# Attention and a gated feed-forward block on one core: bias rows of the first two heads computed in place, the others by DMA, and two loads issued by another engine

## The chip, the cores and the metric

The kernel runs on one core of a Trainium2 chip. A core has TensorE (PE; its weight loads are the row PEld), VectorE (DVE), ScalarE (ACT), GpSimd (POOL) and SyncE (SP), which only issues and waits, and 16 DMA engines. The metric is device time in microseconds: the median of several runs of one launch. The kernel before took 376.75 us (three runs, 376.2 to 377.3).

## The reference

Sixty-four heads (8 batches of 8) of causal attention over 576 positions with head size 64. Each head has a row of selection values s; the running sum of their positive parts is a bias on the scores. The result goes through a gated feed-forward block of width 1536.

```python
scores = scale * np.matmul(q, k.transpose(0, 1, 3, 2))
cum = np.cumsum(np.maximum(s, 0.0), axis=-1)
bias = -(cum[:, :, :, None] - cum[:, :, None, :])
scores = np.where(causal, -1000000000.0, scores + np.minimum(bias, 0.0))
attn = softmax(scores)                       # exp, divided by the sum
x = (attn @ v) rearranged to 4608 tokens x 512
g = x @ w_gate
out = (g * sigmoid(g) * (x @ w_val)) @ w_out
```

## The kernel before

**Scores with the bias inside the product.** A head's q and k are held transposed: 64 partitions of head dimension, 576 positions along the free axis. The other 64 partitions of the same operand tile are free, and four rows of them carry the bias: the running sum, split into a bf16 part and the bf16 rest, against rows of constants. One matmul with a contraction of 128 then gives score plus bias. The operand tiles are KQ[i][r] (kq in the profile). A group of four heads ("head batch" hb) uses the pair KQ[hb % 2]; r = 0 holds heads 0 and 1 of the group side by side, r = 1 heads 2 and 3. With r = 0 the data is in partitions 0 to 63 and the bias rows begin at partition 64; with r = 1 it is the other way round.

**The bias rows.** s (64 heads, one per partition) is loaded by SyncE (L188). VectorE makes, for all heads at once, 8 times the positive part (L226), the running sum c8 (L227, a scan), its bf16 part (L230), the rest (L231) and a copy for the other side (L232), into HL: one partition per head, four rows of two sides. `aug(hb, engs)` (L178 to L186) then moves each head's line of HL into the four rows of its operand by one small DMA, 9 KB per head. The rest of those 64 partitions has to be zero; ScalarE, GpSimd and VectorE fill it at the start (L213 to L220).

**The start.** SyncE issues s, then k and q of head batch 0 in halves ("rows" r = 0, 1); GpSimd issues k and q of batch 1 (L221). A half is cast to bf16 (L247), transposed by TensorE (L293) and copied out of PSUM to KQ (`pe_out`, L305) by ScalarE or VectorE. The order is written out by hand in L905 to L975: fillers for TensorE (`keep_warm`), casts, `aug(0)`, rows of batch 0, the loads of v (`load_v`) and of the weights by GpSimd, `aug(1)`, casts of batch 1, scores of heads 0 to 3 with the transposes of batch 1 between them, `aug(2)`, scores 4 and 5, the products with v (`values`), and so on. After `aug(3)` SyncE issues v of batch 1 and k, q of head batches 4 and 5 (L957 to L959).

**After the start** attention and feed-forward are interleaved. `ffn_items(tt)` (L870) is a generator of steps for 512 tokens: for each of 12 feature tiles a gate block and a value block (L629, four matmuls each), with ScalarE's tanh (L650) and VectorE's `pp` (L652, empties the gate's bank) and `ht` (L663, empties the value's bank); then the output product (L686 or L735). The main loop (L1003 to L1033) counts these steps as items, lets `pump` advance the attention generator in proportion, and calls what was hung on an item by `at_item(n, f)`. Blocks are numbered here as items are: gate block of tile ft is item 2 ft + 1, value block item 2 ft + 2. In the chunks named below, a head's scores are four pieces with their own banks (`score_piece`, L338), followed by ScalarE's exponential (L369).

**What fixes the order.** Each engine runs its instructions in the order in which the program gives them, and waits in order too. Every DMA that SyncE issues goes to one queue (q1 in the profile), all of GpSimd's to another (q0). PSUM has eight banks, chosen at build time (`take`, L120): a block that takes a bank waits for the engine that last emptied it.

Of the kernel before, what the change touches and what calls it, by code (L numbers as in the profile page):

```python
# [12 lines left out]
FP32 = mybir.dt.float32  # L13
BF16 = mybir.dt.bfloat16
# [5 lines left out]
def kernel(  # L20
# [20 lines left out]
    HB = 4  # L41
# [55 lines left out]
    one_s = const.tile([128, 1], FP32)  # L97
    HL = const.tile([BH, 4, 2, S], BF16)
    XR = 3 * TT
# [4 lines left out]
    first = first_sbuf.enter_context(tc.tile_pool(name="first", bufs=1))  # L104
    s_sb = first.tile([BH, S], FP32)
    c8 = first.tile([BH, S], FP32)
    PTP = {0: first, "bufs": 7}
    lower = first.tile([128, 512], BF16)

    with tc.manual_schedule():  # L110
# [25 lines left out]
        def load_one(hb, name, rs=(0, NR), eng=nc.sync):  # L136
            b, g = divmod(hb, 2)
            if rs[0] == 0:
                loaded[name, hb] = raw.tile([128, NR, J, D], FP32, tag="raw" + name, name="raw" + name)
            eng.dma_start(  # L140
                loaded[name, hb][:, rs[0] : rs[1], :, :].rearrange("x r j d -> x r (j d)"),
                SRC[name][0][b, g * HB + 2 * rs[0] : g * HB + 2 * rs[1], :, :].rearrange(
                    "(r e) (p j) d -> (e p) r (j d)", e=2, j=J
                ),
            )
# [28 lines left out]
        def aug_rows(i, r):  # L174
            r0 = 64 * (1 - r)
            return KQ[i][r][r0 : r0 + 64, :, :].bitcast(FP32)

        def aug(hb, engs):  # L178
            for hh in range(HB):
                r, e = divmod(hh, 2)  # L180
                r0 = 64 * (1 - r)
                bh = hb * HB + hh
                engs[hh].dma_start(  # L183
                    KQ[hb % 2][r][r0 : r0 + 4, :, e * S : (e + 1) * S],
                    HL[bh : bh + 1, :, :, :],
                )  # L186

        nc.sync.dma_start(s_sb, s.rearrange("b h n -> (b h) n"))  # L188
        def init_vt(i):
# [3 lines left out]
        for r in range(NR):  # L193
            load_one(0, "k", (r, r + 1))
            load_one(0, "q", (r, r + 1))

        nc.vector.memset(warm, 0.0)
        nc.vector.memset(one_s, 1.0)
        nc.scalar.activation(warm, warm, AF.Exp)
        nc.vector.memset(HL[:, 0:2, 0, :].bitcast(FP32), ONES2)  # L200
        nc.vector.memset(HL[:, 2:4, 1, :].bitcast(FP32), NEGS2)
        make_identity(nc, ident)
# [3 lines left out]
            compare_op=ALU.is_ge, fill=nc.gpsimd.to_reg(MASKED), base=0, channel_multiplier=-1,  # L206
        )

        def pads(i):
            for r in range(2):  # L210
                nc.gpsimd.memset(KQ[i][r][64 * r : 64 * r + 64, :, NR * S :], 0.0)  # L211

        for r in range(2):  # L213
            nc.gpsimd.memset(aug_rows(0, r)[:, 1, :], 0.0)
            nc.scalar.mul(
                KQ[0][r][64 * (1 - r) : 64 * (1 - r) + 64, 0, :],
                one_s[0:64, 0:1].to_broadcast([64, NR * S + 64]), 0.0,
            )
        pads(0)
        nc.vector.memset(aug_rows(1, 0), 0.0)  # L220
        for nm in ("k", "q"):  # L221
            load_one(1, nm, eng=nc.gpsimd)
        init_vt(0)
        pads(1)

        nc.vector.tensor_scalar(s_sb, s_sb, 0.0, 8.0, ALU.max, ALU.mult)  # L226
        nc.vector.tensor_tensor_scan(  # L227
            c8, one_s[0:BH, 0:1].to_broadcast([BH, S]), s_sb, 0.0, ALU.mult, ALU.add
        )
        nc.vector.tensor_copy(HL[:, 0, 1, :], c8)  # L230
        nc.vector.tensor_sub(HL[:, 1, 1, :], c8, HL[:, 0, 1, :])  # L231
        nc.vector.tensor_copy(HL[:, 2:4, 0, :], HL[:, 0:2, 1, :])  # L232

# [650 lines left out]

        def row_half(nm, r, eng):
            for g in range(2):
                pe_transpose_half(0, nm, g, r)
            for g in range(2):
                pe_out(0, nm, g, r, eng)
# [17 lines left out]
        cast_half(0, "q", 0, nc.scalar)  # L907
        aug(0, SP4)
        row_half("k", 0, nc.scalar)
        row_half("q", 0, nc.vector)  # L910
        cast_half(0, "k", 1, nc.scalar)
        cast_half(0, "q", 1, nc.gpsimd)
        nc.gpsimd.memset(aug_rows(1, 1), 0.0)
        load_v(0, range(5), nc.gpsimd)
        w_load("g", 0)
        aug(1, SP4)
        keep_warm(10)
        row_half("k", 1, nc.scalar)
        row_half("q", 1, nc.vector)
        keep_warm(10)  # L920
        cast_one(1, "k", nc.vector)
        cast_one(1, "q", nc.vector)
        for c in range(3):
# [8 lines left out]
        load_one(3, "k", eng=nc.gpsimd)  # L932
        scores(0)
        half_batch("k")
        scores(1)
        half_batch("q")
        scores(2)
        scores(3)
        for nm in ("k", "q"):
            for g in range(2):  # L940
                pe_out(1, nm, g, 1, nc.vector)
        cast_v(0, 4, nc.vector)
        aug(2, SP4)
        cast_one(2, "k", nc.gpsimd)
# [52 lines left out]

        at_item(2, prep_one, 2, 2)
        at_item(8, cast_one, 3, "k", nc.gpsimd)
        at_item(9, cast_one, 3, "q", nc.gpsimd)  # L1000
# [64 lines left out]
```

## Time and profile before

| | us |
|---|---|
| median of 3 runs | 376.75 (376.2 to 377.3) |
| the profiled execution, its own time | 375.79 |
| its span, first to last instruction | 374.0 |
| TensorE busy, 0 to 10 / 10 to 20 / 20 to 30 / 30 to 40 | 7.38 / 8.00 / 9.92 / 8.02 |
| TensorE busy, 40 to 50 / 50 to 60 / 60 to 70 | 9.81 / 9.62 / 9.89 |
| TensorE busy in each 50 us from 100 to 350 | 49.58 to 49.84 |
| VectorE busy, 40 to 50 / 50 to 60 / 60 to 70 / 70 to 80 | 7.52 / 7.21 / 6.91 / 2.85 |

A row of a timeline gives the start and length in us, the engine, the line, the operation, what it writes and reads, the number of merged instructions, and in brackets the idle time of the engine before it and what ended it. In a "waits" line the name after the arrow is what ended the wait. SPq rows are issues by SyncE's queue: their length is the time of issuing, not of the transfer. "Landing" is when a transfer's data is all there.

### The profile page before, as it was taken

Reading aid. Unit: us, or ns where it says so; the run is one execution under the profiler, and the core shown is the slowest. Engines: PE = TensorE matmul, PEld = TensorE weight load, DVE = VectorE, ACT = ScalarE, POOL = GpSimd, SP = SyncE. Lnnn points to the kernel's source line nnn. Section 1 sums busy time; section 2 is a strip of 40 time slices with the busy share of each in tenths; the row PEclk is TensorE's granted clock in tenths of the full one; section 3 lists DMA queues with packets and bytes.
Section 4 is the critical chain, followed back from the end, with each engine's and each line's share of the span. In section 5 each row is a group of like instructions: output and inputs, shape, how many; then the busy total and the mean of one; then the engine's idle time right before and its main releaser. Section 6 shows DMA issues by size and latency. Waiting matters only on the chain.

```text
span 374.0 us, 8759 instructions
## 1 busy us (share of the span) xinstructions
PE 360.7 (96%) x3259; PEld 230.6 (62%) x3300; DVE 289.6 (77%) x578; ACT 240.4 (64%) x471; POOL 212.3 (57%) x325
## 2 busy tenths in 40 slices
PE   7799899999999999999999999999999999999995
PEld 6584456655555556855685559655865585476464
DVE  8968776468995899588967997699858867975984
ACT  8777677698876877588757875686566523323321
POOL 8883555856455647494649464955675516315320
PEclk9999999999999999999999999999999999999999
DMA  7899999799877997896779675984132103002003
GB/s 239 193 258 253 219 257 267 237 303 247 245 186 220 254 262 196 178 281 205 211 167 266 178 182 174 255 206 98 40 119 62 35 19 128 2 0 95 20 0 114
DMA packets 97146, 64.23 MB, mean 172 GB/s; under 512 B 77232, under 2 KB 82736, under 8 KB 97104
## 3 DMA queue, kind: packets, MB, share of 16 engines
q1 hardware_dynamic: 84976, 41.46, 45.2%
q0 software_dynamic: 12128, 22.21, 22.6%
q8 instruction: 26, 0.43, 0.5%
q14 instruction: 16, 0.13, 0.1%
HBM read 37.90 MB, written 19.86 MB: 154 GB/s over the span
## 4 chain that ended last, share of the span: by engine, by line
PE 85%; DMA 6%; POOL 5%; ACT 1%; issue 1%; DVE 1%; DVEq 0%; POOLq 0%; ACTq 0%
PE bank L629 45%; PE bank L735 17%; PE bank L359 10%; PE bank L396 7%; PE bank L686 5%; DMA rawk<-in_k_dram 4%; DMA rawv<-in_v_dram 2%; POOL rawv L157 1%; POOL vt L168 1%; POOL wv L332 1%; ACT pt L369 1%; PE bank L287 0%; POOL rawq L140 0%; ACT kq L314 0%; POOL kq L211 0%
## 5 line engine op out<-in xcount | busy, mean ns | idle before, releaser
L369 ACT ACTIVATE pt<-bank 128x512 bf16<-128x512 f32 (+1 forms) x256 | 120.4, 510 | 31.0 <-PE bank L359 18.2
L629 PE MATMUL bank<-XT,wg 128*128 128x512 bf16 x418 | 110.3, 379 | 1.2 <-DVE pp L652 0.3
L629 PE MATMUL bank<-XT,wv 128*128 128x512 bf16 x412 | 109.3, 379 | 1.1
L650 ACT ACTIVATE th<-bank 128x512 bf16<-128x512 f32 x108 | 64.7, 599 | 55.9 <-PE bank L629 53.6
L652 DVE SCALAR_TENSOR_TENSOR pp<-th,bank 128x512 bf16<-128x512 bf16 x108 | 73.6, 682 | 19.2 <-ACT th L650 18.7
L663 DVE SCALAR_TENSOR_TENSOR ht<-pp,bank 128x512 bf16<-128x512 bf16 x108 | 74.1, 686 | 10.6 <-PE bank L629 0.4
L359 PE MATMUL bank<-kq 128*128 128x128 bf16 (+4 forms) x576 | 75.6, 240 | 1.5 <-DMA kq<-HL 1.0
L672 POOL TENSOR_TENSOR ht<-ht 128x512 bf16<-128x512 bf16 x35 | 40.4, 1154 | 52.2 <-DVE su L670 52.1
L359 PEld LDWEIGHTS <-kq 128*128 128x128 bf16 x576 | 45.8, 98 | 31.5 <-issue 1.9
L629 PEld LDWEIGHTS <-wv 128*128 128x128 bf16 x432 | 38.4, 98 | 36.5 <-issue 0.6
L629 PEld LDWEIGHTS <-wg 128*128 128x128 bf16 x432 | 38.3, 98 | 34.2 <-issue 0.7
L396 PEld LDWEIGHTS <-pt 128*128 128x128 bf16 x960 | 41.9, 98 | 17.2
L374 POOL TENSOR_SCALAR_AFFINE_SELECT pt<-pt 128x512 bf16<-128x512 bf16 x56 | 36.8, 658 | 27.3 <-ACT pt L369 22.7
L396 PE MATMUL bank<-vt,pt 128*128 128x65 bf16 x960 | 47.0, 194 | 0.4 <-POOL vt L168 0.3
L430 POOL DMA_DIRECT2D xs<-ot x24 | 21.7, 905 | 30.0 <-DVE ot L413 27.6
L735 PEld LDWEIGHTS <-ht 128*128 128x128 bf16 x336 | 31.2, 98 | 4.3
L413 DVE TENSOR_TENSOR ot<-bank,rc 128x320 bf16<-128x320 f32 x64 | 31.5, 492 | 2.2
L183 POOL DMA_DIRECT2D kq<-HL x48 | 28.9, 604 | 0.0
L735 PEld LDWEIGHTS <-su 128*128 128x128 bf16 x252 | 23.5, 98 | 3.3
L686 PE MATMUL bank<-wo,ht 128*128 128x512 bf16 x90 | 24.8, 379 | 0.3
L800 POOL TENSOR_TENSOR ysb<-ysb 128x512 f32<-128x512 f32 x12 | 15.2, 1270 | 15.3 <-DVE ysb L794 15.3
L379 POOL TENSOR_SCALAR_AFFINE_SELECT pt<-pt 128x64 bf16<-128x64 bf16 x56 | 14.8, 264 | 15.8 <-ACT pt L369 15.7
(93 smaller groups left out, 384.6 us busy)
## 6 DMA issues: line engine op xcount, KB each, us to landing
out_dram<-ysb POOLq DMA_DIRECT2D x32, 256.0 KB, 4.5
rawv<-in_v_dram SPq DMA_DIRECT2D x28, 256.0 KB
rawk<-in_k_dram SPq DMA_DIRECT2D x12, 576.0 KB
rawq<-in_q_dram SPq DMA_DIRECT2D x12, 576.0 KB
xs<-ot POOLq DMA_DIRECT2D x24, 160.0 KB, 3.5
ks<-ck SPq DMA_DIRECT2D x11, 288.0 KB
qs<-cq SPq DMA_DIRECT2D x11, 288.0 KB
rawk<-in_k_dram POOLq DMA_DIRECT2D x3, 576.0 KB, 7.3
```

The lines of the kernel that those rows point to most:

```text
L359: nc.tensor.matmul(sc[:, o : o + w], T[:, 1, e * S + 128 * tj : e * S + 128 * (tj + 1)], T[:, 0, e * S + lo : e * S + hi], start=not maske ...
L369: nc.scalar.activation(pt[:, c0 : c0 + n], sc, AF.Exp, scale=0.125)
L374: nc.gpsimd.affine_select(pt[:, 1088:1600], pt[:, 1088:1600], pattern=[[0, 4], [1, 128]], compare_op=ALU.is_ge, fill=zreg, base=0, channel ...
L396: nc.tensor.matmul(av[:, bi * (D + 1) : (bi + 1) * (D + 1)], pt[:, c0 : c0 + 128], VT[b % 2][:, tj, h, :], start=(tj == 0), stop=(tj == bi),)
L413: nc.vector.tensor_mul(ot[:, :, e * D : (e + 1) * D], av3[:, :, 0:D], rc[:, :, None].to_broadcast([128, NCH, D]),)
L629: nc.tensor.matmul(view(bs, TT), w[:, c, f0 : f0 + 128], xt[:, c, :], start=(c == 0), stop=(c == 3),)
L650: nc.scalar.activation(th, pg, AF.Tanh, scale=0.5)
L652: nc.vector.scalar_tensor_tensor(pp, in0=th, scalar=1.0, in1=pg, op0=ALU.add, op1=ALU.mult)
L663: nc.vector.scalar_tensor_tensor(hp[:, 2 * k2 : 2 * k2 + 2, :].rearrange("p a n -> p (a n)"), in0=pp, scalar=0.5, in1=pv, op0=ALU.mult, op ...
L672: (nc.vector if ft == NFT - 1 else nc.gpsimd).tensor_sub(hp[:, 1:3, :], hp[:, 1:4:2, :], hp[:, 0:3:2, :])
L686: nc.tensor.matmul(view(pys[ts_], DM), hps[ft // 2][:, 2 * (ft % 2) + half, c0 : c0 + 128], WO[j][:, ft % WKO, :], start=(ft == 0), stop=( ...
L735: nc.tensor.matmul(ps, lhs(p), rhs(p), start=(first and p == 0), stop=(last and p == NP - 1), skip_group_check=True,)
```

## The change

- HL gets 128 partitions. The head's line is now at `hl_row(bh)`: heads 0 to 57 in partitions 70 to 127, the last six heads in 0 to 5. Rows 2 to 57 of s are loaded by SyncE into partitions 72 to 127; rows 0 and 1, each repeated four times, by a DMA that ScalarE issues, into partitions 64 to 71.
- Heads 0 and 1: partitions 64 to 71 of HL hold the sum or the rest, chosen per partition by small role vectors made from the identity, and `sums_rows` writes the operand's rows in the same partitions: two instructions by ScalarE for head 0, two by VectorE for head 1. `aug(0)` moves heads 2 and 3 only. Zero fills are arranged anew; one of GpSimd's clears the in-place rows again before `aug(2)`.
- The last six heads are made later, in seven steps hung on items 13 to 19, from a tile `ends` that SyncE loads in the first step.
- k and q of batch 1 are issued by SyncE right after batch 0. Their casts go to GpSimd; the v loads, the casts of batch 0 and the rows of k and q are put in another order, ten fillers go, and the scores of head 0 come before row q 1.

```diff
-    HL = const.tile([BH, 4, 2, S], BF16)
+    HL = const.tile([128, 4, 2, S], BF16)
...
+        nc.sync.dma_start(s_sb[72:128, :], s_rows[2:58, :])
+        nc.scalar.dma_start(s_sb[64:72, :], s_rows[None, 0:2, :].to_broadcast([4, 2, S]))
...
+        load_qk(1)
...
-            nc.scalar.mul(
-                KQ[0][r][64 * (1 - r) : 64 * (1 - r) + 64, 0, :],
-                one_s[0:64, 0:1].to_broadcast([64, NR * S + 64]), 0.0,
-            )
...
-        for nm in ("k", "q"):
-            load_one(1, nm, eng=nc.gpsimd)
...
+        nc.vector.tensor_copy(HL[up, 0, 1, :], c8[up])
+        nc.vector.scalar_tensor_tensor(
+            HL[up, 1, 1, :], in0=HL[up, 0, 1, :], scalar=b_lo[up], in1=c8[up],
+            op0=ALU.mult, op1=ALU.add,
+        )
+        nc.vector.tensor_copy(HL[up, 2:4, 0, :], HL[up, 0:2, 1, :])
+        def sums_rows(e, eng):
+            for side, a, m in ((1, a_k, e), (0, a_q, 2 + e)):
+                dst = KQ[0][0][up, side, e * S : (e + 1) * S]
...
+        def end_sums(i):
...
+            if i == 0:
+                nc.sync.dma_start(s_end, s_rows[58:, :])
+            elif i == 1:
+                nc.vector.memset(HL[0:n, 0:2, 0, :].bitcast(FP32), ONES2)
+                nc.vector.memset(HL[0:n, 2:4, 1, :].bitcast(FP32), NEGS2)
+            elif i == 2:
+                nc.vector.tensor_scalar(s_end, s_end, 0.0, 8.0, ALU.max, ALU.mult)
+            elif i == 3:
+                nc.vector.tensor_tensor_scan(
...
+            elif i == 4:
+                nc.vector.tensor_copy(HL[0:n, 0, 1, :], c_end)
+            elif i == 5:
+                nc.vector.tensor_sub(HL[0:n, 1, 1, :], c_end, HL[0:n, 0, 1, :])
+            else:
+                nc.vector.tensor_copy(HL[0:n, 2:4, 0, :], HL[0:n, 0:2, 1, :])
...
-        aug(0, SP4)
-        row_half("k", 0, nc.scalar)
-        row_half("q", 0, nc.vector)
-        cast_half(0, "k", 1, nc.scalar)
-        cast_half(0, "q", 1, nc.gpsimd)
-        nc.gpsimd.memset(aug_rows(1, 1), 0.0)
-        load_v(0, range(5), nc.gpsimd)
+        aug(0, SP4, (2, 3))
+        aug(1, SP4)
+        row_half("k", 0)
+        row_out("k", 0, nc.scalar)
+        row_half("q", 0)
+        cast_half(0, "k", 1, nc.gpsimd)
+        init_vt(0)
+        load_v(0, range(3), nc.gpsimd)
+        row_out("q", 0, nc.vector)
+        sums_rows(0, nc.scalar)
+        row_half("k", 1)
+        cast_half(0, "q", 1, nc.scalar)
+        keep_warm(10)
+        sums_rows(1, nc.vector)
+        cast_one(1, "k", nc.gpsimd)
+        cast_one(1, "q", nc.gpsimd)
+        load_v(0, range(3, 5), nc.gpsimd)
         w_load("g", 0)
-        aug(1, SP4)
-        keep_warm(10)
-        row_half("k", 1, nc.scalar)
-        row_half("q", 1, nc.vector)
-        keep_warm(10)
-        cast_one(1, "k", nc.vector)
-        cast_one(1, "q", nc.vector)
+        scores(0)
+        row_half("q", 1)
+        row_out("k", 1, nc.vector)
+        row_out("q", 1, nc.vector)
...
+        nc.gpsimd.memset(KQ[0][0][up, 1, 0 : NR * S].bitcast(FP32), 0.0)
         aug(2, SP4)
...
+        for i in range(7):
+            at_item(13 + i, end_sums, i)
```

## The prediction

> **What bounds the kernel now.** I read the page first (busy time, slices, chain), then busy time by stage, then the timelines of single engines up to 62 us, then the DMA view over short windows.
>
> From the page: TensorE's line of part 1, the slices of TensorE and of DMA, the chain.
>
> ```profile
> PE 360.7 (96%) x3259; PEld 230.6 (62%) x3300; DVE 289.6 (77%) x578; ACT 240.4 (64%) x471; POOL 212.3 (57%) x325
> PE   7799899999999999999999999999999999999995
> DMA  7899999799877997896779675984132103002003
> PE 85%; DMA 6%; POOL 5%; ACT 1%; issue 1%; DVE 1%; DVEq 0%; POOLq 0%; ACTq 0%
> ```
>
> From 60 us on TensorE is never really idle (49.6 to 49.8 of every 50 us up to 350), so the end comes 314 us after whatever TensorE does at 60: what the change is worth is where it puts TensorE at 60. The changed instructions all stand before that. There TensorE does wait, and the DMA engines are full: their share is 1.07 to 1.27 in every 2 us from 28 to 62. TensorE's timeline, three rows (start, length, instruction, idle time before it and what ended that):
>
> ```profile
> 10.91 0.83 PE L359 MATMUL bank<-kq 128*128 128x128 bf16 x8 [0.99 <-DMA kq<-HL]
> 39.92 0.45 PE L287 MATMUL bank<-ident,ck 128*128 128x128 bf16 x5 [1.16 <-POOL ck L246]
> 49.77 1.02 PE L629 MATMUL bank<-XT,wg 128*128 128x512 bf16 x4
> ```
>
> The first is what the change aims at: the first scores wait 0.99 us for bias rows that come by DMA. The third becomes important below.
>
> **The start.** Removed: ScalarE's two zero fills (L215, 2.45 us), which nothing waits for; the bias DMAs of heads 0 and 1; ten of the twenty fillers after the first 32 (0.73), which stand in idle time. Added on ScalarE: the issue of eight rows of s (0.59, by SyncE's for s); its table load then ends at 2.7, ahead of the first cast at 4.69. VectorE: one zero fill of 1.07 (to 2.1), five tiny instructions (0.2 each, like the reciprocals: 3.2), two memsets of HL (4.4), then as before L226 (4.95), the scan (6.35), the cast (6.85), 0.75 for the difference (7.6), the copy (8.15, 7.40 before). Row q 0 follows (1.43) to 9.55; ScalarE's two new rows (0.66 each, by the 128x576 casts; 0.45 by VectorE's least, 0.7 by L314) need the difference and end at 8.9. First scores at 9.6 instead of 10.91: **1.3 earlier**.
>
> Not all of it lasts. VectorE then has two new rows (0.27 each by L232's rate, 0.6 by L226's; I take 0.43) and the k 1 copies (1.43) ahead of q 1 and the eight copies of L316, loses two casts to GpSimd (1.88), and ends the copies at about 18.9 instead of 18.03. Banks wait for them, so TensorE reaches the first values (19.53 before) only 0.3 earlier. k 1 and q 1, issued by SyncE at 3.5 and 3.95 (by GpSimd at 4.51 and 5.41 before), free GpSimd, but two casts (1.14 each) now stand ahead of the last two v loads, which go 0.4 later, as do the gate weights (0.6); k 3 is issued at 22.4 instead of 22.81.
>
> **The new wait on SyncE.** aug(2), at 15.60 to 19.72 before, now waits for the new zero fill on GpSimd (0.55, hidden in GpSimd's own wait of 1.36 for k 2 before 24.94), which stands behind the issue of k 3: 23.75. Queued behind aug(2) are aug(3), v 1, k 4, q 4, k 5, q 5. Eight issues at 0.62 to 0.65 put the first v 1 load at 28.9 instead of 24.54. GpSimd's transfers have the DMA engines to themselves that much longer, so k 3 comes a little sooner and the 1.16 us wait may go; v 1 comes later, and its chunk 3, for which TensorE waited 0.28 at 53.66, is again about when it is needed. aug(2) itself lands about 29 (4.4 after its issue), ahead of the scores at 32.55. Alone, I put the sum of all this at zero, -1.5 to +0.8.
>
> **The new work on VectorE, and what it waits for.** end_sums makes HL of the last six heads between the feed-forward blocks: two memsets, 0.54 each, then 0.55, 1.35, 0.45, 0.75, 0.54 by the rows of L200, L226 to L232: 4.7 us where VectorE has 2.5 to 2.8 idle in 10. Its first instruction with data needs the six rows of s, and their DMA (13.8 KB) is issued by SyncE **behind q 5**. How long that takes is told by SyncE's and GpSimd's timelines:
>
> ```profile
> 24.54 18.74 SPq L157 DMA_DIRECT2D rawv<-in_v_dram  x5
> 45.04 0.45 SPq L140 DMA_DIRECT2D rawq<-in_q_dram  x1
> 46.11 0.41 SPq L140 DMA_DIRECT2D rawq<-in_q_dram  x1
> 54.18 9.56 SPq L157 DMA_DIRECT2D rawv<-in_v_dram  x5
> 56.88 1.15 POOL L246 CAST cq<-rawq 128x1152 bf16<-128x1152 f32 x1 [1.45 <-DMA rawq<-in_q_dram]
> ```
>
> q 4, issued at 45.04, lands at 56.85; k 5 and q 5 stand behind it. Are later ones held up? The v 2 rows, issued from 54.18, are the only packets of 256 B about. The DMA view's packet lines for 54 to 56, 58 to 60 and 60 to 62:
>
> ```profile
> DMA packets 355, 0.59 MB, mean 293 GB/s; under 512 B 4, under 2 KB 178, under 8 KB 355
> ...
> DMA packets 877, 0.73 MB, mean 364 GB/s; under 512 B 619, under 2 KB 633, under 8 KB 877
> ...
> DMA packets 1506, 0.43 MB, mean 217 GB/s; under 512 B 1476, under 2 KB 1476, under 8 KB 1505
> ```
>
> They hardly move until k 5 and q 5 are through: SyncE's transfers go in the order of issue. k 4 to q 5 are 2.36 MB; the queue's bytes from 48 on (0.03, 0.35, 0.38, 0.41, 0.59, 0.55 MB per 2 us, v taken out) sum to 2.31 at 60, so q 5 lands at 60 to 61. The changed kernel has the same bytes ahead of it, with the engines full in both, so the six rows land at **60.3** (58.3 if GpSimd's transfers have gained 2 us, 62.5 if SyncE's late v 1 leaves gaps).
>
> VectorE meets this wait at about 48 and is then blocked, and with it every pp and ht. VectorE's rows that stand behind it (before):
>
> ```profile
> 47.45 0.69 DVE L652 SCALAR_TENSOR_TENSOR pp<-th,bank 128x512 bf16<-128x512 bf16 x1 [1.14 <-ACT th L650]
> 49.03 0.69 DVE L663 SCALAR_TENSOR_TENSOR ht<-pp,bank 128x512 bf16<-128x512 bf16 x1
> 49.63 0.68 DVE L652 SCALAR_TENSOR_TENSOR pp<-th,bank 128x512 bf16<-128x512 bf16 x1
> ```
>
> In the changed order L226's like stands between the first and the second of these. The ht at 49.03 empties the bank of the value block of feature tile 7 (item 16, on TensorE at 45.97); the gate block of tile 9 (item 19, at 49.77) writes that bank. So TensorE stops there.
>
> **The sum.** Landing 60.3 + 0.55 + 0.69 + 0.1 for two hand-overs = 61.65, against 49.77: +11.9. Behind it VectorE is still short: by the same durations the pp of gate tile 8 is done 3.46 after the landing (score chunk 1 of head 12 wants it at 3.07), the ht of value tile 9 at 7.5 (wanted at 6.9), the pp of gate tile 11 0.25 late: +1.35. The 0.28 wait goes: -0.28. Together **+13.0**, on the profiled execution's 375.8 (span 374.0 and 1.8 around it): **388.8**; that execution lies 1 us under the median of 376.75, inside the runs' 376.2 to 377.3 give or take 0.4. What the start gained does not enter: TensorE waits anyway.
>
> Two rules of the Trainium skill bear on this. "DMA: Bandwidth & Descriptors", section "Latency and other measured facts", has about 0.8 us as the least for a small HBM transfer; by that alone the rows would be there at 48, and the time would be about 376, but the row above has 11.8 us for q 4 behind its queue. "TensorE: Matmul & The Clock Gate", Part 1, says that an idle window of about 3.4 us puts the matmul clock at half until as much activity has passed; an estimate from it is up to 1.7 us more, so up to 390.5. This trace shows the slow matmuls only at the start.
>
> In rows of this case that start is 32 fillers in 3.33 us (104 ns each) and later ten in 0.73; 32 times the difference of some 44 ns bounds it at +1.4, below at nothing. I take nothing, as VectorE's 1.35 covers most of it.
>
> **The rivals.**
> 1. *The six rows pass the loads.* A small DMA is then like aug's: 4.4 us median from issue to landing. Issued at 47.2, landed at 51.6: gate tile 9 at 52.95, +3.2 + 1.35 - 0.28 = +4.3: **380.1**. Against it: the 256 B packets held up to 58. For it: no small transfer behind large ones is in this trace.
> 2. *The rows are there in time*, and v 1's lateness eats the early start: **375.8**, within 1. It needs an issue by 43.5; before, SyncE was held by its full queue until 43.39, and v 1 starts later now.
> 3. *The other side, faster:* as 2, but v 1 is in time too, because GpSimd's transfers run ahead by more than 1 us. Then the 1.3 at the start or the 1.16 at 39.92 is kept, not both: **374.4**. It decides where chunk 3 of v 1 lands before 51.5.
> 4. *The early rows do not help the first scores* (row q 0 behind VectorE's longer work): with the main case this changes nothing, 388.8, as TensorE waits at gate tile 9.
>
> **How the numbers follow.** Forecast (4 within it) 0.84; rival 1 0.08; rival 2 0.04; rival 3 0.04. Landing from 58.3 to 62.5 gives 386.8 to 391.0, with the slow clock 392.4. To hold 8 in 10 the forecast's own spread is enough; I widen it at the low end to 384.5 for a queue that runs faster while TensorE stands: 384.5 to 392.4. A measurement tells about 0.3% (1.1 us) from no change: faster 0.04, same 0.04, slower 0.92.
>
> **What would show it.** Right: a wait of some 12 us on VectorE, ended by the DMA of s, with TensorE idle from about 48.5 to 61.5 at gate tile 9; first scores at 9.6; first v 1 load on SyncE near 29; k 4 landed before that wait ends; the stages from 62 on as long as before. Wrong: VectorE's wait under 5 us (rival 1 or 2), or TensorE stopped elsewhere, or the six rows landed with k 4 rather than q 5.

## The result, and the profile after

The changed kernel takes **391.57 us** (median of 4 runs, 390.31 to 393.28); beside it the kernel before took 376.48 (4 runs, 374.72 to 377.3). The ratio is 1.041, with a 95% interval of 1.038 to 1.045: slower by about 15 us, where 13 had been forecast. The profiled execution took 391.6 (span 389.7, 15.7 more than before).

The page of the changed kernel: TensorE's line of part 1, the slices of TensorE and of the granted clock, and the chain by engine and by line.

```profile
PE 365.0 (94%) x3290; PEld 231.8 (59%) x3290; DVE 295.5 (76%) x592; ACT 238.4 (61%) x469; POOL 213.4 (55%) x325
PE   6999904999999999999999999999999999999995
PEclk9899975999999999999999999999999999999999
PE 88%; DMA 4%; DVE 3%; ACT 2%; issue 1%; POOL 1%; SPq 0%; DVEq 0%; ACTq 0%; POOLq 0%
PE bank L681 46%; PE bank L787 16%; PE bank L411 10%; PE bank L448 7%; PE bank L738 5%; DMA ends<-in_s_dram 3%; DVE kq L368 2%; DMA rawk<-in_k_dram 1%; ACT pt L421 1%; PE bank L339 1%; DVE ht L715 1%; DVE pp L704 1%; PE bank L497 1%; ACT kq L366 1%; PE bank L353 0%
```

A slice is 9.74 us. The sixth (48.7 to 58.5) is a 0 on TensorE, and the row of the granted clock falls to 7 in it and to 5 in the seventh. The chain has a link that the kernel before had not, the DMA of `ends`, 3% of the span. From the eighth slice on TensorE's row is all nines up to the last, as it was before.

The view of waits from 40 to 75 us (who waited for whom: total, times, longest) names both ends of it:

```profile
PE bank L681 <- DVE ht L715: 14.1, 1, 14.1
DVE ends L274 <- DMA ends<-in_s_dram: 13.5, 1, 13.5
```

The timelines of VectorE and then of TensorE show the order (start, length, instruction, idle time before it and what ended that):

```profile
47.95 0.83 DVE L368 COPY kq<-bank 64x640 bf16<-64x640 bf16 x1
62.26 0.45 DVE L274 TENSOR_SCALAR ends<-ends 6x576 f32<-6x576 f32 x1 [13.48 <-DMA ends<-in_s_dram]
62.74 0.69 DVE L715 SCALAR_TENSOR_TENSOR ht<-pp,bank 128x512 bf16<-128x512 bf16 x1
```

```profile
49.03 0.39 PE L411 MATMUL bank<-kq 128*128 128x128 bf16 x4
63.48 1.86 PE L681 MATMUL bank<-XT,wg 128*128 128x512 bf16 x4 [14.06 <-DVE ht L715]
65.14 1.78 PE L681 MATMUL bank<-XT,wv 128*128 128x512 bf16 x4
```

VectorE stands in front of one instruction on six partitions (L274). The `ht` behind it waits for nothing of its own, and gate tile 9 (63.48 now, 49.77 before) needs the bank that this `ht` empties. The two blocks after the stop take 1.86 and 1.78 us instead of 1.03.

SyncE's timeline (issues, with the time that each took):

```profile
25.25 5.66 SPq L190 DMA_DIRECT2D kq<-HL  x8
31.16 13.54 SPq L161 DMA_DIRECT2D rawv<-in_v_dram  x5
50.55 1.14 SPq L144 DMA_DIRECT2D rawq<-in_q_dram  x1
51.74 0.36 SPq L269 DMA_DIRECT2D ends<-in_s_dram  x1
```

The six rows (13.5 KB) are issued at 51.74, after VectorE has begun to wait at 48.78, and land at 62.2; q 5, issued just ahead of them, lands at 62.0.

**The account of the span, +15.7.** The scores at 49.03 start 0.22 earlier than before. Gate tile 9 is 13.71 late. The first score chunk of head 13 starts at 69.87 (55.16 before) and is 14.71 late: 1.56 more for the slow blocks, and 0.56 less because v 1, late or not, is there when it is wanted. Nothing more is lost until 312, where one wait of 0.90 is new; 0.1 is added at the end.

### The profile page after: what moved, and what is told of

Its sections match the earlier page's. It is cut to its first block, busy times and chain, and to the rows that moved or that the text cites. A ratio compares the mean times of both kernels' runs of the same rounds, so it can differ in the third digit from the quotient of the medians.

```text
span 389.7 us, 8797 instructions
## 1 busy us (share of the span) xinstructions
PE 365.0 (94%) x3290; PEld 231.8 (59%) x3290; DVE 295.5 (76%) x592; ACT 238.4 (61%) x469; POOL 213.4 (55%) x325
## 4 chain that ended last, share of the span: by engine, by line
PE 88%; DMA 4%; DVE 3%; ACT 2%; issue 1%; POOL 1%; SPq 0%; DVEq 0%; ACTq 0%; POOLq 0%
PE bank L681 46%; PE bank L787 16%; PE bank L411 10%; PE bank L448 7%; PE bank L738 5%; DMA ends<-in_s_dram 3%; DVE kq L368 2%; DMA rawk<-in_k_dram 1%; ACT pt L421 1%; PE bank L339 1%; DVE ht L715 1%; DVE pp L704 1%; PE bank L497 1%; ACT kq L366 1%; PE bank L353 0%
## 5 line engine op out<-in xcount | busy, mean ns | idle before, releaser
L681 PE MATMUL bank<-XT,wg 128*128 128x512 bf16 x432 | 112.2, 381 | 14.4 <-DVE ht L715 14.1
L681 PE MATMUL bank<-XT,wv 128*128 128x512 bf16 x432 | 111.6, 381 | 0.1
L738 PE MATMUL bank<-wo,ht 128*128 128x512 bf16 x96 | 25.8, 379 | 0.0
```

The lines of the kernel that those rows point to most:

```text
L681: nc.tensor.matmul(view(bs, TT), w[:, c, f0 : f0 + 128], xt[:, c, :], start=(c == 0), stop=(c == 3),)
L738: nc.tensor.matmul(view(pys[ts_], DM), hps[ft // 2][:, 2 * (ft % 2) + half, c0 : c0 + 128], WO[j][:, ft % WKO, :], start=(ft == 0), stop=( ...
```

## The experiments

The theory, W, is that the price is VectorE's in-order wait for rows that land behind q 5 in SyncE's queue. There are two rivals: the rearranged start and the late v 1 carry the loss (S), or the DMA engines are so full that any small transfer would have been as late (E). The first four kernels ran together, beside a median of 376.0 for the kernel before. Times in brackets are the profiled execution's span.

**The rows loaded at the start.** The same buffer, filled right after q 1:

```diff
         load_qk(1)
+        ends = [yp.tile([128, 2, DM], FP32, tag="y", name="ends").rearrange("p a n -> p (a n)")[0 : BH - 58, 0:S]]
+        nc.sync.dma_start(ends[0], s_rows[58:, :])
...
-                nc.sync.dma_start(s_end, s_rows[58:, :])
```

> The six rows of s are loaded by SyncE right after q 1, in the first microseconds, into the same buffer; the six steps of VectorE stay at items 14 to 19. Theory W (VectorE's in-order wait for rows that land behind q 5 is the cost): the wait of 13.5 us and TensorE's stop of 14.06 go whole, gate tile 9 stands at 49.5 (49.03 + 0.4, as everything ahead of it is 0.2 earlier than in the kernel before), and the time falls by 13 to 15 us, to 376.5 to 379.5. Within that: with chunks 3 and 4 of v 1 cast as late as in the changed kernel (done at 54.4 and 56.5, wanted at about 53.5 and 54.7) TensorE waits about 2 us there, 378.5; if VectorE's 4.7 us of work are the next limit, up to 1.35 us, 377.7; neither, 376.3. Rival S (the new work and the later start and loads carry half of the loss or more, and the wait only hides them): 383 or more.

379.63 us (377.9), ratio 1.011 (1.008 to 1.014). This is 0.1 above the 376.5 to 379.5 expected, and far from the 383 or more of S: about 12 of the 15 us go with one transfer moved, as W has it. TensorE around gate tile 9 and value tile 10:

```profile
50.63 1.02 PE L675 MATMUL bank<-XT,wg 128*128 128x512 bf16 x4 [0.62 <-DVE ht L709]
54.98 0.28 PE L442 MATMUL bank<-vt,pt 128*128 128x65 bf16 x4 [0.87 <-POOL vt L172]
55.53 0.19 PE L442 MATMUL bank<-vt,pt 128*128 128x65 bf16 x1 [0.28 <-POOL vt L172]
```

What is left is small and has three places: 0.62 for VectorE's added work at gate tile 9, 1.15 for the casts of v 1, and waits after 60 that the next runs sort out.

**Another queue, same moment.**

```diff
-                nc.sync.dma_start(s_end, s_rows[58:, :])
+                nc.scalar.dma_start(s_end, s_rows[58:, :])
```

> Only the issuer of the six rows' DMA is changed: ScalarE at the same item 13, instead of SyncE. Theory Q (the rows are late because SyncE's queue passes them on in the order of issue): issued near 46, landed within 5 us of it (the 4.4 us median of the bias rows' DMAs), so VectorE waits 0 to 3 us, and the time is 376.5 to 381.5. Rival E (the 16 DMA engines are full, so that any small transfer of this moment waits for the loads in them, whichever queue it comes from): landed at 58 or later, TensorE stopped for 9 us or more, 387 to 391.

379.26 us (376.9), ratio 1.009 (1.007 to 1.011). ScalarE's timeline has the issue, VectorE's has no wait:

```profile
43.72 0.32 ACTq L269 DMA_DIRECT2D ends<-in_s_dram  x1
```

```profile
49.42 0.45 DVE L274 TENSOR_SCALAR ends<-ends 6x576 f32<-6x576 f32 x1
```

The rows land at 48.7, 5.0 us after their issue, while the DMA engines are as full as in the changed kernel (a share of 1.17 from 43.5 to 50; there 1.12 from 51.7 to 62.2). So E falls: not the engines, the queue made the rows late. Two things changed with the queue, though: the place in the order, and the time of issue, since SyncE comes to this issue only at 51.74. Of the 13.5 us that the rows are later (62.2 against 48.7), 8.0 are SyncE's issue, 5.5 the longer way. The Trainium skill, "DMA: Bandwidth & Descriptors", section "Queues, rings and completion order", says that SyncE and ScalarE each have a row of rings on the same 16 engines, and that an engine takes turns between rows; the run agrees with it: 5.0 us from issue to landing against 10.5 on SyncE.

**The rows late, the work later.**

```diff
-            at_item(13 + i, end_sums, i)
+            at_item((13, 14, 27, 27, 30, 30, 33)[i], end_sums, i)
```

> The rows' DMA stays on SyncE at item 13, behind q 5; VectorE's steps that need them move from items 15 to 19 to items 27 (first step, scan), 30 (copy, difference) and 33 (copy), among the output blocks. Theory W: rows that land late cost nothing if nobody meets them; without the stop item 27 is at about 62, when the rows (landed at 60 to 62) are there or short of it: VectorE waits under 1.5 us, TensorE less, and the time is that of the version with the early rows, within 1.5: 376 to 379.5. Rival S: 383 or more, as work and loads are the same.

381.04 us by the median (378.73 to 383.98; the profiled execution's span is 377.9), ratio 1.015 (1.011 to 1.019). The spread is wide, and the time is above the 376 to 379.5 expected; four of the six executions have a mean granted clock of 0.985 to 0.996, the profiled one 1.0, so its trace cannot show what those four lost. It shows that the stop is gone. The same instruction, in the view of the tile `ends`:

```profile
L269 SPq DMA_DIRECT2D ends<-in_s_dram x1: 641/641/641, 50.9 to 50.9; - x1
L274 DVE TENSOR_SCALAR ends<-ends x1: 449/449/449, 65.0 to 65.0; 6x576 f32<-6x576 f32 x1
```

The rows land at 61.6, about as late as in the changed kernel; VectorE comes to them at 65.0 and waits for nothing. What a late transfer costs depends on when the first instruction that needs it comes up in its engine's order.

**The kernel before, with the wait alone.** One DMA and one multiplication on VectorE, whose result nothing uses:

```diff
+                nc.sync.dma_start(ends[0], s.rearrange("b h n -> (b h) n")[58:, :])
...
+                nc.vector.tensor_scalar(ends[0], ends[0], 0.0, 8.0, ALU.max, ALU.mult)
...
+        at_item(13, end_wait, 0)
+        at_item(15, end_wait, 1)
```

> The kernel before with two things added and nothing else: SyncE's DMA of six rows of s at item 13 (behind q 5), and one VectorE multiplication on them at item 15; the result of it is not used. Theory W: the rows land at 60 to 62, VectorE and with it TensorE stand from about 49 until then, and this alone gives most of the loss: +12 to +15 on the kernel before, 388 to 391.5. Rival S (the start's rearrangement and the later v 1 and k 3 make the rows late or add the loss): +3 or less, under 380. If the slow matmul clock follows the idle time and not the changed start, the first blocks after the stop take about 1.8 us instead of 1.03 here too.

390.2 us (388.4), ratio 1.038 (1.036 to 1.040). Its SyncE, VectorE and TensorE:

```profile
46.24 1.58 SPq L1006 DMA_DIRECT2D ends<-in_s_dram  x1
```

```profile
61.06 0.45 DVE L1008 TENSOR_SCALAR ends<-ends 6x576 f32<-6x576 f32 x1 [13.06 <-DMA ends<-in_s_dram]
```

```profile
48.25 0.39 PE L359 MATMUL bank<-kq 128*128 128x128 bf16 x4
62.28 1.86 PE L629 MATMUL bank<-XT,wg 128*128 128x512 bf16 x4 [13.64 <-DVE ht L663]
63.94 1.91 PE L629 MATMUL bank<-XT,wv 128*128 128x512 bf16 x4
```

This settles W against S: with the old start, the old v 1 and none of the other work, one transfer and one multiplication bring +14.2 us. It also parts issue from landing: issued at 46.24, 5.5 us earlier than in the changed kernel, the rows landed at 61.0, only 1.2 earlier. The place behind q 5 sets the landing, not the time of issue.

**The slow clock.** Is it the idle time that makes the blocks after the stop slow? Filler matmuls ahead of gate tile 9, into a bank that is free then (160, then 215); they add only work that nothing uses:

```diff
             for ft in range(NFT):
+                if tt == 0 and ft == 9:
+                    last = max((x for x in bank if released[x] < OPEN), key=lambda x: released[x])
+                    for _ in range(160):
+                        nc.tensor.matmul(view(last, 128), ident, ident, start=True, stop=True)
```

> The changed kernel itself, with 160 filler matmuls (128x128 by 128x128, 73 ns each, 11.7 us) ahead of gate tile 9, into the bank of the scores before it, so that TensorE works through most of the stop. They add work in idle time only. Theory C (the slow gate and value block after the stop, 1.86 and 1.78 us instead of 1.03, come from the idle time's effect on the granted clock): both blocks take 1.03, gate tile 9 starts where it did (63.5), and the time falls by about 1.5 us, to 390.0 from 391.6. Rival: the blocks are slow for another reason (VectorE's and ScalarE's backlog empties their banks late), and they stay at 1.8 and 391.6.

> As the run with 160 fillers, but with 215 of them: they took 57 ns each, ended at 59.5 and left 3.25 us of idle time, after which the clock was at half from about 62.8. At 57 ns 215 take 12.2 us, from 50.4 to 62.7, about when gate tile 9 can start. Theory C (the granted clock falls about 3.3 us after TensorE falls idle, and the slow blocks come from that alone): the clock is 1.00 from 48 to 70, gate and value tile 9 take 1.03 each, and the next scores come 1.72 us after gate tile 9 as in the kernel before, not 3.28 or 3.02; 390 by the median. Rival (backlog of VectorE and ScalarE): blocks of 1.8 us at a clock of 1.00, and 391.5.

With 160: 392.22 us (391.0), no gain; with 215: 390.3 (389.3). TensorE with 160, and its window of 62 to 64 (busy times, then the granted clock, here 0.79, DMA share, GB/s); then the same of 215:

```profile
50.43 9.09 PE L702 MATMUL bank<-ident 128*128 128x128 bf16 x160 [1.38 <-ACT pt L421]
62.78 1.52 PE L681 MATMUL bank<-XT,wg 128*128 128x512 bf16 x3 [3.25 <-DVE ht L719]
64.10 1.91 PE L681 MATMUL bank<-XT,wv 128*128 128x512 bf16 x4
```

```profile
62.00:64.00 2.00, 1.13 (x3) 0.48 (x4) 1.97 (x4) 0.00 (x0) 0.00 (x0) 0.79 1.17 239
```

```profile
51.64 12.16 PE L702 MATMUL bank<-ident 128*128 128x128 bf16 x215 [1.38 <-ACT pt L421]
63.64 1.03 PE L681 MATMUL bank<-XT,wg 128*128 128x512 bf16 x3
64.50 1.03 PE L681 MATMUL bank<-XT,wv 128*128 128x512 bf16 x4
```

```profile
62.00:64.00 2.00, 2.00 (x34) 1.84 (x33) 2.00 (x3) 0.00 (x0) 0.00 (x0) 1.00 0.89 198
```

The first set of fillers ended at 59.5 and missed its aim: the fillers took 57 ns each, not 73. It shows something else instead: a gap of 3.25 us was enough to lose the clock. By half microseconds, the granted clock fell 3.6 us after the last matmul, at 63.2, 0.4 after gate tile 9 had begun, and was back at 66.6, 3.8 us after that beginning. In the changed kernel it fell 3.6 us after the last matmul and came back 3.2 us after the restart; in the kernel before with the wait alone both took 5.1. The Trainium skill, "TensorE: Matmul & The Clock Gate", Part 1, gives a window of about 3.4 us both ways; these rows lie around it, from 3.2 to 5.1.

With no gap the blocks take 1.03 each, and the next scores come 1.73 after gate tile 9, instead of 3.28. So the slow clock costs 1.5 us, and follows the idle time, not VectorE's backlog; the kernel before with the wait alone has the same slow blocks, without the added work that would lie behind them. The second set was too long by 1.2 us (the `ht` ended at 62.5, the fillers at 63.6), which gives VectorE that much time and takes as much of the gain. In the time itself little is seen: 390.3 is 14.4 above the kernel before beside it (375.91), where the changed kernel was 15.1 above its own, and the rows landed 0.9 earlier in this execution. The 1.5 rests on the trace.

**The remainder.** The next versions start from the one with the early rows; each adds one step to the version above it. First GpSimd's zero fill moves ahead of its casts of v 0, with the call for head 1's scores, which it has to follow. Then VectorE's steps move to items 25.5, 27, 28.5, 30 and 33. Then head 1's bias rows come by DMA again, as they did before the change; for that GpSimd zeroes head 1's half of the rows at the start, and the later fill is half as long. The cuts show the main lines of each.

```diff
+        nc.gpsimd.memset(KQ[0][0][up, 1, 0 : NR * S].bitcast(FP32), 0.0)
         for c in range(3):
             cast_v(0, c, nc.gpsimd)
```

```diff
-        for i in range(1, 7):
-            at_item(13 + i, end_sums, i)
+        for i, n in enumerate((14, 25.5, 27, 28.5, 30, 33), 1):
+            at_item(n, end_sums, i)
```

```diff
-        aug(0, SP4, (2, 3))
+        aug(0, SP4, (1, 2, 3))
...
-        sums_rows(1, nc.vector)
```

> The version with the early rows, and GpSimd's zero fill of the k side moved from behind the issue of k 3 (23.4) to right behind the gate weights (about 16), where the scores of head 1 are done (13.7). aug(2) then waits for the scores of heads 2 and 3 alone (20.0), aug(3) for those of heads 4 to 7 (25.1), and the first load of v 1 is issued near 26 instead of 31.2. Theory L (the two waits for chunks 3 and 4 of v 1, 0.87 and 0.28, are the late zero fill's): they go, the span falls by 1.1 against the version with the early rows, 378.5 by its median. If chunks 3 and 4 are held up by VectorE's and GpSimd's casts running side by side instead, as GpSimd's five casts of v 1 took 3.9 us there and 2.9 before, the waits stay and the time is that of the early rows, 379.6.

> As the one before, and VectorE's five steps on the rows go from items 15 to 19 to the output blocks (items 25.5, 27, 28.5, 30 and 33). Theory V (VectorE's added work between items 15 and 19 delays gate tile 9 by its ht, 0.62 idle): the idle time at gate tile 9 goes, another 0.5 to 0.9 us: 377.6 to 378.0. What is left against the kernel before (376.0) is then the start (TensorE 0.4 behind at the scores at 49) and one wait of 0.9 us near 300, of which the cause is open. Rival: the output blocks need VectorE as much (waits of 0.25 to 0.28 for XT and ot when the work stood at items 27 to 33), no gain, 378.5.

> As the one before, and the bias rows of head 1 by DMA again (only head 0's are made in place): VectorE loses two instructions of 0.88 and 1.30 at 10.5 to 12.6, ahead of twelve copies that TensorE's banks wait for. Theory D (the start loses behind the first scores what it gains ahead of them, through VectorE): the copies end about 1.5 to 2 us earlier than 21.15 and the first values come near 20 instead of 21.45; but the wait for k 3, 1.16 in the kernel before at 39.92, then comes back in part, so that the scores at 49 are at most 0.4 earlier: 377.2 to 378. Rival: head 1's rows by DMA land too late for its scores (12.68), and the start is no faster: same as the one before or up to 1 us slower.

378.41 us (376.5), 378.39 (376.4) and 377.76 (376.0), beside 375.76: ratios 1.007 (1.004 to 1.010), 1.007 (1.005 to 1.009) and 1.005 (1.004 to 1.007). The medians hardly tell them apart (the second missed its 377.6 to 378.0); the traces do. In the first, v 1 is issued at 25.86 instead of 29.87, and yet TensorE waits for its casts as with the early rows alone (0.88 and 0.28): theory L, by which the late zero fill makes these waits, falls. In the second the 0.88 and the 0.62 at gate tile 9 are gone, though only VectorE's work was moved. GpSimd's last three casts, of the first version and of the second:

```profile
53.40 2.47 POOL L172 CAST vt<-rawv 128x512 bf16<-128x512 f32 x3
```

```profile
52.85 1.72 POOL L172 CAST vt<-rawv 128x512 bf16<-128x512 f32 x3
```

The same casts take 0.75 us longer while VectorE runs the difference and the copy of HL beside them. VectorE's two instructions are longer as well: 1.15 and 0.82 there, 0.74 and 0.44 in the changed kernel after its stop. The Trainium skill, "GPSIMD Engine Reference", section "1. Specifications", names instructions of VectorE with two inputs from SBUF as one cause of contention between the two engines; the difference is such an instruction, and the rows agree, though no run parts it from the copy. From the scores at 49 to the first of head 13 TensorE needs 7.42 us in the first version and 5.92 in the second (5.91 in the kernel before): VectorE's work costs 1.5 us between the blocks, so theory V (the added work there holds TensorE up) is right for that stretch. The two medians agree even so: the second version's profiled execution reached the scores at 49 later by 0.44, and a wait of 0.31 is new in its output blocks. The third gained nothing at the start: its first values come at 21.59, because its copies waited 1.14 for the cast of k 1 on GpSimd.

**The start.** That cast back on VectorE; then k 3's load ahead of two weight loads; then 20 more fillers (12 ahead of the transposes of k 0's second half, 18 instead of 10 behind).

```diff
-        cast_one(1, "k", nc.gpsimd)
+        cast_one(1, "k", nc.vector)
```

```diff
+        load_one(3, "k", eng=nc.gpsimd)
         for nm in ("g", "v"):
             w_load(nm, 1, 0)
-        load_one(3, "k", eng=nc.gpsimd)
```

```diff
+        keep_warm(12)
         row_half("k", 1)
...
-        keep_warm(10)
+        keep_warm(18)
```

> As the version with head 1's bias rows by DMA, and the cast of k 1 on VectorE again, where 1.66 us stood idle at 11.4; on GpSimd it stood behind three issues of v loads, and VectorE's copies of k 1 waited 1.14 us for it at 15.6. Theory D (the early first scores are lost again through the casts that were moved to GpSimd): the copies end near 19, the first values come at 19.5 to 20.2 instead of 21.5, that is 1.5 to 2 us earlier. Theory K (behind that the third batch of k decides: GpSimd casts it at 39.1 at the earliest, 38.7 in the kernel before): of those 1.5 to 2 us TensorE stands about 1.2 again at the transposes of k 3 (40.0), and at the scores at 49 only 0.4 to 0.6 is left: 377.3 by the median. If k 3 has come sooner too, 376.2.

> As the one before, and GpSimd issues the load of k 3 ahead of the two weight loads that stood before it, 1.5 us earlier. Theory K: k 3 is cast up to 1.5 us earlier and TensorE's wait at the transposes of k 3 goes or is under 0.3: another 0.5 to 1.0 us, 376.3 to 376.8, level with the kernel before (375.8) but for the wait of 0.9 near 300. If the weights that are now behind k 3 are late, or if the engines are so full that k 3 lands no sooner: no gain, 377.3, with a wait at the first block that uses those weights.

> As the version with k 3 first, and 20 more filler matmuls at the start: 12 ahead of the transposes of k 0's second half, where TensorE stood 0.2 to 1.9 us, and 18 instead of 10 behind them. Theory F: the ten fillers that the change took out of the start were not free. Of eleven profiled executions with the changed start six have a granted clock of 0.5 for some 3 us between 8 and 16, of two with the old start (20 fillers there) none. Then the clock is 1.00 up to 20 here, the matmuls of 10 to 16 are as long as in the kernel before, and the median comes down by 0.3 to 0.8 us, to 376.0 to 376.5, level with the kernel before (375.9). Rival: the clock falls here too (it comes from the stalls behind the first scores, at 12 to 16, which no filler covers), and the time stays at 376.8. A third: the fillers delay the transposes of k 0 by up to 1 us, and the first scores come at 10.8 or later instead of 10.0 to 10.4: 377.3.

378.27 us (374.5), 376.81 (375.1) and 376.70 (374.1), beside 375.91 and, for the last, 375.64: ratios 1.004 (1.001 to 1.008), 1.003 (1.001 to 1.006) and 1.004 (1.002 to 1.006). The first missed its 377.3 and has a wide spread, 375.9 to 381.16; the last missed its 376.0 to 376.5. By the traces theory D (the start loses behind the first scores, through the casts moved to GpSimd, what it gained ahead of them) holds for two steps together: head 1's rows by DMA alone gave nothing, and with the cast of k 1 back on VectorE as well the copies end at 19.83 and the first values come at 20.16. The cast alone was not run. Theory K (k 3 is the next limit) falls: in the first of the three versions TensorE does not wait for k 3, whose cast starts at 37.59 (38.72 before). So the lower median of the second cannot be put down to k 3's earlier load: the profiled executions of the two have spans of 374.5 and 375.1, the other way round. Why k 3 comes sooner is open; v 1's load was nearly as early there as in the kernel before (24.98 and 24.54). The scores at 49 come at 48.35 in the first version and at 47.85 in the last, 0.90 and 1.40 earlier than before the change.

On fillers, theory F says that the ten that the change took out of the start were not free. The granted clock of the changed kernel in the three windows from 8 to 14 (0.66, 0.50 and 0.99, behind the five engines):

```profile
8.00:10.00 2.00, 1.21 (x11) 1.04 (x12) 1.93 (x4) 1.73 (x3) 1.94 (x4) 0.66 0.94 364
10.00:12.00 2.00, 2.00 (x16) 1.67 (x16) 1.94 (x4) 0.56 (x1) 2.00 (x3) 0.50 0.38 88
12.00:14.00 2.00, 1.84 (x21) 1.28 (x20) 1.51 (x3) 1.69 (x4) 1.96 (x3) 0.99 0.75 200
```

Six of eleven profiled executions with the changed start had such a stretch of about 3 us at half speed, none of two with the old start, and none in the last version. The mean clock of the executions that were not profiled adds to this. Some 3.4 us at half speed in 376 lower the mean by 0.0045 (an estimate), and the profiled executions with such a stretch and no stop have 0.995, those without one 0.998 to 1.0. At 0.996 or below are 10 of 69 executions of the kernel before, 25 of 65 of the eight versions with ten fillers and no stop, and 2 of 12 of the last. So the old start loses the clock too, the changed one more often, and twelve executions are too few to say what the fillers gave back. The median moved by 0.1, and F stays open. The clock is not what is left of the loss: among the executions above 0.996 the last version still has 376.35, the kernel before beside it 375.59.

No version beats the kernel before. The last one is 1.40 ahead at 49 us and 0.1 behind at the end. On the way it meets a wait of 0.36 for VectorE in the output blocks, and one of 0.90 near 297. This last loss is the same in all that have VectorE's new work, and begins with GpSimd's issue of the outputs of head pair 30, here of the kernel with ScalarE's DMA and then of the kernel before:

```profile
297.13 0.89 POOL L482 DMA_DIRECT2D xs<-ot  x1 [4.08 <-DVE pp L704]
```

```profile
293.67 0.89 POOL L430 DMA_DIRECT2D xs<-ot  x1 [2.51 <-DVE ot L413]
```

It comes 1.87 us after VectorE's multiplication `ot` instead of 0.30, right after a later instruction, the `pp` that the profile names. GpSimd's masks come late behind it, and TensorE waits 0.90 for a head's values. In the changed kernel the same issue is at 309.95 with the same 4.08 us of idle time before it; the kernel with the wait alone has no such loss. Why this one issue waits for the `pp` is open: the order of VectorE's instructions around it is the same in both, and no run tried it.

## Why the prediction was right, step by step

The forecast was 388.8 (+13.0), within 384.5 to 392.4; measured 391.57, +15.1 by the medians, +15.7 by the spans.

- **The mechanism**, from the wait on VectorE to the bank of gate tile 9, was right in each link, and is shown from both sides: taken away it gives 12 us back, put into the kernel before it costs 14.2. Rival 1 was wrong in its premise that a small DMA passes the loads of its own queue, and right for another queue (5.0 us; it took 4.4).
- **The landing, 60.3** came at 62.2; the term was 1.9 short. In the kernel before with the wait alone it is 61.0, so 0.7 is the count of bytes. The other 1.2 go with the changed start and the later v 1, the gap that the upper end of 62.5 allowed for, and partly with this one execution: three others with these first instructions landed the rows at 61.3 to 61.6. The first v 1 load, forecast near 29, was issued at 31.16 here (29.8 to 30.0 in those three): the zero fill on GpSimd ended at 25.2 instead of 23.75, and the eight issues took 0.71 each. Gate tile 9 is 13.7 late instead of 11.9.
- **VectorE's shortage behind the stop, +1.35**: none of its own shows. In its place stands the slow clock, +1.5, for which the sum took nothing because the shortage would cover it. It was the other way round: slow matmuls leave VectorE its time. Whether the shortage would show with the clock kept stays open, since the 215 fillers gave VectorE 1.2 us of their own; without a stop it is real (+1.5 with the early rows). The bound of +1.4 was right as a size, but does not follow from the rows given for it: 104 less 73 ns is 31 a filler, not 44, and makes +1.0. With the 57 ns that fillers took at full speed in the stop it would be 47 and +1.5.
- **v 1's wait of 0.28 goes**: right, with 0.28 more beside it. Without the stop these waits would have been 1.15, and not from the late load but from casts that share their time with VectorE. The range of -1.5 to +0.8 for the start and v 1 alone is not contradicted: with VectorE's work out of the way and v 1 early, TensorE is 0.42 behind the kernel before at head 13. The other losses of the versions without a stop are VectorE's work and later waits (0.31, 0.90).
- **The first scores at 9.6**: wrong, 11.36 in this execution and 10.62 or 10.63 in seven others with these first instructions. The forecast took VectorE's instructions at the old durations. Two rows of the kernel with ScalarE's DMA:

```profile
4.22 1.27 DVE L234 TENSOR_SCALAR s_sb<-s_sb 64x576 f32<-64x576 f32 x1
10.62 0.82 PE L411 MATMUL bank<-kq 128*128 128x128 bf16 x8 [1.65 <-DVE kq L368]
```

  The multiplication of s by 8 took 1.27 instead of 0.55 beside GpSimd's zero fill (4.07 to 5.17), and the cast of the sums 0.74 instead of 0.45 beside GpSimd's cast of k 0; HL was done at 9.0 instead of 8.15, and the copies of row q 0, which the scores wait for, behind it. ScalarE's new rows took 0.86 instead of 0.66. In the versions with head 1's rows by DMA, whose fills run at other times (one to 4.53), the multiplication took 0.60 to 0.63. In all these rows VectorE's instruction ends 0.3 us after the one of GpSimd that ran when it began: the multiplication at 5.49 after 5.17 and at 4.85 after 4.53, the cast at 7.65 after 7.33, and in the kernel before the multiplication of 0.55, at 4.17 after 3.86. So GpSimd's instructions seem to hold VectorE's up, though no run was made for it. The rest of the way to 11.36 has another cause, which the forecast left out:

```profile
7.60 1.14 POOL L308 CAST ck<-rawk 128x576 bf16<-128x576 f32 x1 [1.74 <-DMA rawk<-in_k_dram]
8.79 1.17 PE L353 MATMUL bank<-ident,ck 128*64 128x128 bf16 x9 [1.86 <-POOL ck L308]
11.36 1.16 PE L411 MATMUL bank<-kq 128*128 128x128 bf16 x8
```

  In this execution GpSimd waited 1.74 for the second half of k 0, TensorE 1.86 for its cast, and then the transposes, the fillers and the scores themselves ran at a lowered clock, with no idle time between them.
- **The first values 0.3 earlier**: 1.3 later (20.84), in the version with ScalarE's DMA 1.9 (21.45). The term that failed is the end of the copies, 18.9: there they end at 21.1, 0.9 from the late row q 0 and 1.3 from head 1's two new rows, for which the forecast took 0.43 each:

```profile
10.50 0.88 DVE L254 TENSOR_SCALAR kq<-HL,a_k,roles 64x576 bf16<-64x576 bf16 x1
11.31 1.30 DVE L254 TENSOR_SCALAR kq<-HL,a_q,roles 64x576 bf16<-64x576 bf16 x1
```

  In the changed kernel's own execution these two took 0.43 and 0.44; the copies end at 20.52, 1.0 late from q 0 and 0.49 more from a wait for transposes that stand behind the late scores.
- **Ten fillers at nothing**: the changed start lost the clock more often than the old one, 25 of 65 executions against 10 of 69; whether the fillers do it is open, see F.
- **k 3's wait may go**: it went, and its 1.16 paid for the late values; so the scores at 49 were 0.22 early in spite of a start that lost 1.3. The reason given, the later v 1, is not shown: the wait is also gone where v 1 is issued at 24.98.
- **The stages after 62 as long as before**: right but for the 0.90 at 312, which nothing in the forecast spoke of.

The stop came as forecast and for the reason forecast; that the sum lies 2.7 us under the spans' difference is nearly all two terms, the landing (1.9 short) and the late wait (0.9, not in the sum). That the slow clock cost about what the shortage was put at (1.5 and 1.35) is luck.

## What to carry to other kernels

Price work hung into a tuned stretch by its first wait, and only then by its length: ask which queue brings its data, what stands ahead of it there, and which engine meets the wait in order. Here 13.5 KB behind 2.3 MB in one queue were as late as the megabytes. Loading them early, or by another queue, or using them later each took away the stop. After such a stop add the clock: here the granted clock fell 3.6 to 5.1 us after the last matmul, it came back 3.2 to 5.1 us after the restart, and that cost 1.5 us.

## What the runs showed of the hardware

- 13.5 KB behind 2.3 MB on SyncE's queue landed 14.8 us after an issue at 46.24 and 10.5 after one at 51.74; on ScalarE's queue, with equally full DMA engines, 5.0 after its issue.
- A gap of 3.25 us on TensorE lost the granted clock; one of 1.38 ahead of the fillers did not. It fell 3.6 us after the last matmul in two executions and 5.1 after it in a third, and was back 3.2 to 5.1 us after the restart. At the start it was lost in six profiled executions without any single gap above 1.9. The slow stretch after the stop cost 1.5 us.
- A cast on GpSimd (128x512) took 0.57 us where VectorE had neither the difference nor the copy of HL, and 0.82 beside them (three in 1.72 and in 2.47).
- At the start a multiplication on VectorE (64x576), begun at 4.22 to 4.25, took 1.27 us where GpSimd had a zero fill running to 5.17, and 0.60 to 0.63 where it had one to 4.53 or 4.54: it ended 0.3 after the fill both times.
